# Moving output-block matmuls ahead of two f tiles, and one accumulating DMA over all tap pairs

## The chip, the core and the metric

The kernel runs on one core of a Trainium2 chip. The metric is the device time of one execution in microseconds (us); it is shown as the median of several runs. The core's engines are named as in the profile: PE (TensorE matmuls), PEld (its weight loads), DVE (VectorE), ACT (ScalarE), POOL (GpSimd) and SP (SyncE, which here only issues DMAs). POOL also issues DMAs.

## What is computed

The reference has two stages. Shapes: x is 8 x 4096 x 192, weight_gen is 8 x 4096 x 8 heads x 7 taps, w_in is 192 x 2048, w_out is 2048 x 192, all float32.

```python
w = softmax(weight_gen, axis=taps)                      # 7 taps
out[b, s, h, g] = sum_k w[b, s, h, k] * x_pad[b, s + k, h, g]   # causal, 6 zero rows ahead
h = out.reshape(32768, 192) @ w_in
g = h - np.tanh(h)
result = g @ w_out
```

## The kernel before

The 32,768 tokens are cut into 32 tiles (n = 0 to 31) of 1,024 tokens. A tile passes through these steps, several tiles being in flight at once.

1. **Weights.** SP loads weight_gen (L98) and x with its halo rows (L112). ACT takes the exponential (L145), DVE sums, inverts and scales (L159, L168, L174, L198). The scaling uses a PSUM bank as scratch space.
2. **Products.** `products(n)` (L204) multiplies x with each of the seven taps on POOL (L223). Taps 0, 2, 4 go to the three planes of `even`, taps 1, 3, 5 to the three planes of `odd`, tap 6 to `last`, all bf16. After the planes are written, POOL issues a DMA (L240) that adds `odd` onto `even` in SBUF (`accum_op=add`), so that the next step has fewer groups to add. From which tile on, and how much of the planes, is set by `PLAIN`, `PART` and `ACC` (L46 to L48): tiles 0 and 1 have no DMA; tiles 2 to 5 (`PART`) send it after tap 3 and over two pairs of planes, so that five groups remain (tap 4, two summed pairs, tap 5, tap 6); tiles 6 to 31 send it after tap 5 and over `ACC` = 4,096 of the 4,608 elements of a partition, so that four groups remain and, for the third 64-column chunk of the 192 columns, a fifth: the part of tap 5 that the DMA left out.
3. **Convolution sums.** `conv_sums(n)` (L259) adds the groups on PE by matmuls with an identity (L276), which also transpose, into PSUM: one buffer `pc` for chunks 0 and 1, a second for chunk 2. ACT (L302) and DVE (L300) copy them to SBUF as `convT`, bf16.
4. **First matmul.** `gemm1(n, f)` (L314) makes one of 16 f tiles (128 columns of w_in by 1,024 tokens) by six matmuls (L319) into a PSUM buffer `ph` of two banks. ACT takes the tanh from it into `th` (L330); DVE subtracts (L331) into `gt`, which frees `ph`.
5. **Second matmul.** `gemm2(i, f0, f1)` (L340) makes an output block of 128 tokens as a sum over the f tiles f0 to f1. Its 128-row contraction is split into two row tiles of 64 that run side by side: the first half of block i goes to one of two PSUM banks, `obank0` or `obank1`, and at the same time the second half of block i-1 to the other. So each f tile is two matmuls (L353), and 16 f tiles are 32. When block i-1 is complete, ACT copies it out (L372); the next block that begins in that bank waits for that copy.

In PSUM two banks are the obanks, and three buffers of two banks each form one pool (`psum_h`, bufs=3, L60), which `ph` and `pc` take in turn. A new `ph` or `pc` therefore waits for the buffer that was taken three allocations before it.

The order on each engine is the order in which the code is written (`tc.manual_schedule()`). The main loop (L509 to L573) goes over n from 1. For p = 0 to 7 it writes gemm1 of f tiles 2p and 2p+1 of tile n, then `out_block(n, p)`, which is gemm2 of block p of tile n-1. At p = 6 the convolution sums of tile n+1 are interleaved with the output block. Between p = 6 and p = 7 stand the sums of chunk 2, and then the first two f tiles of output block 7 (`out_block(n, 7, 0, 2)`, L562), f tiles 14 and 15 of gemm1, and the rest of block 7 (L569). At p = 0 `products(n + 2)` is written too; its first product waits for the subtraction of f tile 1 (`behind=last_sub[0]`, "pace").

At i = 1 (the second output block) a manual dependency (L363) makes the first matmul of the second row tile wait for the ACT instruction kept in `g1_act` (L328): the tanh of f tile 2. At the last block there is one like it.

Of the kernel before, what the change touches and what calls it, by code (L numbers as in the profile page):

```python
# [8 lines left out]
FP32 = mybir.dt.float32  # L9
BF16 = mybir.dt.bfloat16  # L10

ACT = mybir.ActivationFunctionType
# [4 lines left out]
def kernel(  # L17
# [8 lines left out]
    nc = tc.nc  # L26

    B, S, D = x.shape
# [3 lines left out]
    P = nc.NUM_PARTITIONS  # L32
    R = P // 2
    HALO = K - 1

    J = 8
# [6 lines left out]
    NC = D // R  # L43
    GC = G // NC
    NPAIR = K // 2
    ACC = NPAIR * J * D - J * R  # L46
    PLAIN = (0, 1)
    PART = (2, 3, 4, 5)  # L48
    assert S % TOK == 0 and D % R == 0 and H * GC == R and F % P == 0
    assert NFT == 2 * J, "one token block of the second matmul per pair of f tiles"  # L50

# [14 lines left out]
    obank = [psum_o.tile([P, 512], FP32, name=f"obank{i}", tag=f"obank{i}") for i in range(2)]  # L66
    zero = const.tile([1, D], FP32, name="zero")
    nc.vector.memzero(zero[:])

    x_of = {}  # L70
    wg_of = {}
# [4 lines left out]
    prods_of = {}  # L76
    conv_of = {}
    g_of = {}
    last_act = {}
    g1_act = {}  # L80
    last_sub = {}
    last_exp = {}
    last_conv = {}
# [2 lines left out]
    def order(inst, other, reason):  # L86
        tc.add_manual_dep(
            inst.ins,
            other.ins.name,
            mybir.DependencyInfo(mybir.DependencyClass.Sync, mybir.DependencyReason.DATA),  # L90
            reason=reason,
        )
# [111 lines left out]
    def products(n, taps=None, sums=None, hooks={}, behind=None):  # L204

        x_t = x_of.pop(n)
        wsm, wsm_v, e_t, zr = wsm_of.pop(n)
        if e_t is not None:
            scale(nc.gpsimd, wsm[:], e_t, zr[:])

        even = ppool.tile([P, NPAIR, NC, J, H, GC], BF16, name="even")
        odd = ppool.tile([P, NPAIR, NC, J, H, GC], BF16, name="odd")
        last = ppool.tile([P, NC, J, H, GC], BF16, name="last")
        dst = {}
        for i in range(NPAIR):
            dst[2 * i] = even[:, i]
            dst[2 * i + 1] = odd[:, i]
        dst[K - 1] = last[:]
        if -1 in hooks:
            hooks[-1]()  # L220
        for eng, k, j0, j1 in taps or [(nc.gpsimd, k, 0, J) for k in range(K)]:
            w = wsm_v if eng is nc.vector else wsm[:]
            mul = eng.tensor_mul(  # L223
                dst[k][:, :, j0:j1].rearrange("p c j h g -> p j h c g"),
                x_t[:, k + j0 : k + j1, :].rearrange("p j (h c g) -> p j h c g", h=H, c=NC),
                w[:, j0:j1, :, k : k + 1]
                .rearrange("p j h (k o) -> p j h k o", o=1)
                .to_broadcast([P, j1 - j0, H, NC, GC]),
            )
            if k == 0 and behind is not None:  # L230


                order(mul, behind, "pace")
            if j1 == 1:
                first_halo[0] = mul
            if (k, n in PART) in ((3, True), (K - 2, False)) and n not in PLAIN:


                acc = 2 * J * D if n in PART else ACC
                nc.gpsimd.dma_start(  # L240
                    out=even[:].rearrange("p i c j h g -> p (i c j h g)")[:, 0:acc],
                    in_=odd[:].rearrange("p i c j h g -> p (i c j h g)")[:, 0:acc],
                    accum_op=mybir.AluOpType.add,
                    max_dma_last_dim=4096,
                )
            if k in hooks:
                hooks[k]()

        if n in PLAIN:
            prods_of[n] = [[dst[k] for k in (sums or range(K))]] * NC  # L250
        elif n in PART:
            prods_of[n] = [[dst[4], even[:, 0], even[:, 1], dst[5], last[:]]] * NC
        else:
            groups = [last[:]] + [even[:, i] for i in range(NPAIR)]
            prods_of[n] = [
                groups + ([odd[:, NPAIR - 1]] if c == NC - 1 else []) for c in range(NC)
            ]

    def conv_sums(n, parts, pcs, home=None):  # L259

# [53 lines left out]
    def gemm1(n, f):  # L314
        convT = conv_of[n]
        ph = psum_h.tile([P, 2, HT], FP32, name="ph", tag="ph")
        for c in range(NC):
            for r in range(2):
                nc.tensor.matmul(  # L319
                    ph[:, r, :],  # L320
                    lhsT=w_in[r * R : (r + 1) * R, c, f * P : (f + 1) * P],
                    rhs=convT[r * R : (r + 1) * R, c, :],
                    start=(c == 0),
                    stop=(c == NC - 1),
                )
        th = tpool.tile([P, TOK], FP32, name="th")
        ph_f = ph[:].rearrange("p r t -> p (r t)")
        g1_act[0] = last_act.get(0)  # L328
        gt = gpool.tile([P, TOK], BF16, name=f"gt{f}", tag=f"gt{f}")
        last_act[0] = nc.scalar.activation(out=th[:], in_=ph_f, func=ACT.Tanh)  # L330
        last_sub[0] = nc.vector.tensor_sub(gt[:], ph_f, th[:])  # L331
        g_of.setdefault(n, []).append(gt)

    LAST = (NTOT - 1) * J
    LEAD = 5
    LATE = (1, 2, 3, 4, 5, 6)
    half = {}
    out_of = {}

    def gemm2(i, f0=0, f1=NFT, between=lambda f: None):  # L340

        ops = []
        for r, blk in ((0, i), (1, i - 1)):
            if not 0 <= blk < LAST:
                continue
            n, j = divmod(blk, J)
            if r == 0 and f0 == 0:
                half[blk] = obank[blk % 2]
            ops.append((r, n, j, half[blk]))
        for f in range(f0, f1):  # L350
            for r, n, j, po in ops:
                col = (j % 2) * HT + (j // 2) * P
                mm = nc.tensor.matmul(  # L353
                    po[:, 0:D],
                    lhsT=g_of[n][f][r * R : (r + 1) * R, col : col + P],
                    rhs=w_out[r * R : (r + 1) * R, f, :],
                    start=(r == 0 and f == 0),
                    stop=(r == 1 and f == NFT - 1),
                )
                if r == 1 and f == 0 and i in (1, LAST):  # L360


                    order(mm, g1_act[0] if i == 1 else last_act[0], "row tiles in one bank")  # L363
            between(f)
        if i > 0 and f1 == NFT:
            blk = i - 1
            n, j = divmod(blk, J)
            po = half.pop(blk)
            if j == 0:
                out_of[n] = opool.tile([P, J, D], FP32, name="out_sb")  # L370
            out_sb = out_of[n]
            last_act[0] = nc.scalar.activation(out=out_sb[:, j, :], in_=po[:, 0:D], func=ACT.Copy)  # L372
            if j == J - 1:
                out_of.pop(n)
                g_of.pop(n)
                nc.sync.dma_start(
                    out=out[n * TOK : (n + 1) * TOK, :].rearrange("(p j) e -> p j e", p=P),
                    in_=out_sb[:],
                )
# [126 lines left out]
    def out_block(n, p, f0=0, f1=NFT, between=lambda f: None):  # L506
        gemm2((n - 1) * J + p, f0, f1, between)

    for n in range(1, NTOT):  # L509
        for p in range(J):  # L510
            more = n < NTOT - 1
            if more and p == 6:
                break
            gemm1(n, 2 * p)
            gemm1(n, 2 * p + 1)
            if n == 1:

                if p == 0:
                    load_wg(5)
                if p <= 1:  # L520
                    softmax_sum(3, p * JH, (p + 1) * JH)
                elif p <= 3:
                    softmax_recip(3, (p - 2) * JH, (p - 1) * JH)
                else:
                    softmax_sum(4, (p - 4) * JH, (p - 3) * JH)
                if p == 2:
                    softmax_exp(4)
                if p == 3:
                    wsm_of[3] = (softmax_tile(), None, e_of[3], zr_of[3])
                    products(3)  # L530
            elif n + 3 < NTOT:
                if p == 0:
                    softmax_exp(n + 3)
                if p == 0 and n + 4 < NTOT:
                    load_wg(n + 4)
                if 1 <= p <= 2:
                    softmax_sum(n + 3, (p - 1) * JH, p * JH)
                if 3 <= p <= 4:
                    softmax_recip(n + 3, (p - 3) * JH, (p - 2) * JH)
            out_block(n, p)  # L540
            if p == 0 and 1 < n < NTOT - 2:
                products(n + 2, behind=last_sub[0])
            if p == 0 and n + 3 < NTOT and n not in LATE:
                load_x(n + 3)
# [14 lines left out]
        some(conv_sums(n + 1, ((2,),), pcs), K * 4 * JH)  # L559


        out_block(n, 7, 0, 2)  # L562
        conv_out(n + 1, ((2,),), pcs, nc.vector)
        if n + 3 < NTOT:

            softmax_norm(n + 3, pcs[0][:, 0])
        gemm1(n, 14)
        gemm1(n, 15)
        out_block(n, 7, 2)  # L569
        if n in LATE:  # L570


# [37 lines left out]
```

## Time and profile before

| what | value |
|---|---|
| median of 7 runs | 756.95 us (756.25 to 758.35) |
| the profiled execution: its own time | 756.88 us |
| its span, first to last instruction | 755.1 us |
| granted TensorE clock | 1.000 |
| busy: PE / DVE / POOL / ACT | 97% / 92% / 89% / 83% of the span |
| idle time of PE in the span | 20.8 us, of which the startup up to 40 us holds nearly all |
| matmuls | 14,784: 7,936 of gemm2 (L353), 3,072 of gemm1 (L319), 3,520 of the sums (L276), 256 of the last tile's own output (L390) |
| DMAs `even<-odd` | 26 of 1,024 KB and 4 of 768 KB |

The span is what lies between the first and the last instruction; the execution's own time is 1.8 us longer. A busy PE is not a PE at its peak: a matmul's busy time includes its passage through the pipeline, so short waits of PE do not show as idle time. They show as a longer distance between the starts of two matmuls.

### The profile page before, as it was taken

The numbers are of one execution on the slowest core, as the hardware profiler recorded it, in microseconds if no ns is written. First come the engines' busy times: TensorE is split into PE (matmuls) and PEld (weight loads), VectorE is DVE, ScalarE is ACT, GpSimd is POOL, SyncE is SP. The second block draws the span as 40 slices with busy tenths as digits, with TensorE's granted clock in tenths as the row PEclk, the third lists the DMA queues.
The fourth block names the chain that finished last, engine by engine and source line by source line (L and its number), as shares of the span: only waits on it lengthen the run. The fifth ranks groups of instructions, "written<-read, shape, count | busy, mean of one in ns | idle before, by whom it ended". The sixth has DMA issues, their size and how long they took to land.

```text
span 755.1 us, 32326 instructions
## 1 busy us (share of the span) xinstructions
PE 734.3 (97%) x14784; PEld 579.0 (77%) x14784; DVE 695.5 (92%) x740; ACT 625.1 (83%) x839; POOL 670.7 (89%) x264
## 2 busy tenths in 40 slices
PE   3899999999999999999999999999999999999997
PEld 2487878877777877787878777777777777777777
DVE  7989999999999999999999999999999999998893
ACT  4888888888888888888888888888888888888883
POOL 8999999999999999999999999999999999999000
PEclk9999999999999999999999999999999999999999
DMA  8935444466546665554666544666544666542312
GB/s 229 221 67 172 154 146 107 124 185 179 159 136 170 185 184 143 138 137 148 179 185 172 117 133 149 172 185 184 113 130 149 169 185 173 123 111 63 79 45 86
DMA packets 25943, 111.08 MB, mean 147 GB/s; under 512 B 4703, under 2 KB 9551, under 8 KB 21838
## 3 DMA queue, kind: packets, MB, share of 16 engines
q1 hardware_dynamic: 14718, 77.03, 28.3%
q0 software_dynamic: 11088, 31.99, 24.8%
q8 instruction: 115, 1.88, 1.0%
q14 instruction: 22, 0.18, 0.1%
HBM read 54.52 MB, written 25.17 MB: 106 GB/s over the span
## 4 chain that ended last, share of the span: by engine, by line
PE 80%; POOL 17%; DMA 2%; issue 1%; ACT 0%; DVE 0%; POOLq 0%
PE obank L353 37%; PE ph L319 36%; POOL even L223 7%; POOL odd L223 6%; PE pc L276 5%; POOL last L223 2%; PE po L390 1%; DMA even<-odd 1%; POOL wsm L198 0%; POOL w_in L432 0%; DMA wg_t<-in_weight_gen_dram 0%; POOL even L240 0%; POOL w_out L419 0%; ACT e_t L145 0%; DVE out_sb L404 0%
## 5 line engine op out<-in xcount | busy, mean ns | idle before, releaser
L331 DVE TENSOR_TENSOR gt<-ph,th 128x1024 bf16<-128x1024 f32 x512 | 602.4, 1219 | 35.4 <-ACT th L330 32.5
L330 ACT ACTIVATE th<-ph 128x1024 f32<-128x1024 f32 x512 | 497.3, 1022 | 71.8 <-PE ph L319 69.0
L353 PE MATMUL obank<-w_out,gt 64*128 64x192 bf16 x7936 | 407.9, 243 | 0.6 <-ACT th L330 0.4
L353 PEld LDWEIGHTS <-gt 64*128 64x128 bf16 x7936 | 356.4, 94 | 49.7 <-ACT th L330 0.8
L319 PE MATMUL ph<-convT,w_in 64*128 64x512 bf16 x3072 | 385.1, 378 | 4.6 <-DVE gt L331 2.5
L223 POOL TENSOR_TENSOR even<-x_t,wsm 128x1536 bf16<-128x1536 f32 x93 | 285.1, 3065 | 15.2 <-DVE gt L331 15.0
L223 POOL TENSOR_TENSOR odd<-x_t,wsm 128x1536 bf16<-128x1536 f32 x93 | 284.8, 3062 | 0.0
L319 PEld LDWEIGHTS <-w_in 64*128 64x128 bf16 x3072 | 177.5, 94 | 108.3 <-issue 19.5
L372 ACT ACTIVATE out_sb<-obank 128x192 f32<-128x192 f32 x248 | 82.0, 331 | 36.8 <-PE obank L353 30.0
L223 POOL TENSOR_TENSOR last<-x_t,wsm 128x1536 bf16<-128x1536 f32 x32 | 106.7, 3334 | 0.0
L276 PE MATMUL pc<-ident,even 64*128 64x64 bf16 x2256 | 63.0, 192 | 1.2 <-DMA even<-odd 0.9
L276 PEld LDWEIGHTS <-even 64*128 64x128 bf16 x2304 | 60.0, 96 | 2.3 <-DMA even<-odd 1.0
L240 POOL DMA_DIRECT2D even<-odd x30 | 36.1, 1205 | 9.3 <-POOL odd L223 9.3
L276 PE MATMUL pc<-ident,last 64*128 64x64 bf16 x752 | 27.4, 191 | 9.2 <-POOL last L223 9.2
L302 ACT ACTIVATE convT<-pc 128x1024 bf16<-128x1024 f32 (+1 forms) x33 | 32.7, 993 | 2.8 <-PE pc L276 2.8
L276 PEld LDWEIGHTS <-last 64*128 64x128 bf16 x768 | 23.5, 96 | 9.4 <-POOL last L223 9.2
L159 DVE TENSOR_REDUCE zsum<-e_t 128x32 f32<-128x224 f32 (+1 forms) x61 | 23.7, 388 | 2.9 <-ACT e_t L145 2.9
L300 DVE CAST convT<-pc 128x512 bf16<-128x512 f32 x30 | 20.7, 690 | 4.5 <-PE pc L276 2.8
L145 ACT ACTIVATE e_t<-wg_t 128x448 f32<-128x448 f32 x32 | 18.5, 577 | 6.7 <-DMA wg_t<-in_weight_gen_dram 6.7
L168 DVE RECIPROCAL zr<-zsum 128x32 f32<-128x32 f32 (+1 forms) x58 | 20.3, 350 | 0.0
L198 DVE TENSOR_TENSOR wsm<-e_t,pc 128x448 f32<-128x448 f32 x28 | 17.4, 622 | 2.9
L276 PE MATMUL pc<-ident,odd 64*128 64x64 bf16 x400 | 14.5, 199 | 1.1 <-POOL odd L223 0.7
(28 smaller groups left out, 77.1 us busy)
## 6 DMA issues: line engine op xcount, KB each, us to landing
x_t<-in_x_dram SPq DMA_DIRECT2D x31, 1344.0 KB, 9.5
even<-odd POOLq DMA_DIRECT2D x26, 1024.0 KB, 8.9
out_dram<-out_sb SPq DMA_DIRECT2D x31, 768.0 KB, 7.3
wg_t<-in_weight_gen_dram SPq DMA_DIRECT2D x32, 224.0 KB, 9.9
even<-odd POOLq DMA_DIRECT2D x4, 768.0 KB, 7.4
x_t<-in_x_dram SPq DMA_DIRECT2D x1, 768.0 KB
w_out<-in_moe_w_out_dram POOLq DMA_DIRECT2D x1, 768.0 KB, 8.8
out_dram<-out_sb SPq DMA_DIRECT2D x4, 192.0 KB, 2.6
```

The costliest lines, as they stand in the source:

```text
L159: nc.vector.reduce_sum(out=zsum_of[n][:, j0 * H : j1 * H], in_=e_of[n][:, j0:j1].rearrange("p j h k -> p (j h) k"), axis=AX.X,)
L168: nc.vector.reciprocal(zr_of[n][:, j0 * H : j1 * H], zsum_of[n][:, j0 * H : j1 * H])
L223: mul = eng.tensor_mul(dst[k][:, :, j0:j1].rearrange("p c j h g -> p j h c g"), x_t[:, k + j0 : k + j1, :].rearrange("p j (h c g) -> p j h ...
L240: nc.gpsimd.dma_start(out=even[:].rearrange("p i c j h g -> p (i c j h g)")[:, 0:acc], in_=odd[:].rearrange("p i c j h g -> p (i c j h g)" ...
L276: nc.tensor.matmul(pc[r][:, col : col + R] if home else pc[:, r, col : col + R], lhsT=prods[c][gi][r * R : (r + 1) * R, c, 2 * j : 2 * j + ...
L300: eng.tensor_copy(out, pc[:, :, 0:cols].rearrange("p r (cj t) -> p r cj t", t=R))
L302: last_conv[0] = nc.scalar.activation(out=out, in_=pc[:, :, 0:cols].rearrange("p r (cj t) -> p r cj t", t=R), func=ACT.Copy,)
L319: nc.tensor.matmul(ph[:, r, :], lhsT=w_in[r * R : (r + 1) * R, c, f * P : (f + 1) * P], rhs=convT[r * R : (r + 1) * R, c, :], start=(c == ...
L330: last_act[0] = nc.scalar.activation(out=th[:], in_=ph_f, func=ACT.Tanh)
L331: last_sub[0] = nc.vector.tensor_sub(gt[:], ph_f, th[:])
L353: mm = nc.tensor.matmul(po[:, 0:D], lhsT=g_of[n][f][r * R : (r + 1) * R, col : col + P], rhs=w_out[r * R : (r + 1) * R, f, :], start=(r == ...
L372: last_act[0] = nc.scalar.activation(out=out_sb[:, j, :], in_=po[:, 0:D], func=ACT.Copy)
```

## The change

Four things change.

- `FILL`: ahead of f tile 14, four f tiles (eight matmuls) of output block 7 instead of two.
- `AHEAD`: from n = 2 on, three f tiles (six matmuls) of output block 0 stand between f tiles 0 and 1 of gemm1; the other 13 follow f tile 1.
- The accumulating DMA covers all three pairs of planes in tiles 7 to 31, as three pieces of 1,536 elements per partition where there were two of 2,048; the fifth group of chunk 2 goes. Tile 6 moves from this kind to `PART`.
- The manual dependency at i = 1 waits for a new ACT instruction (`probe`), which copies one column of the `ph` of f tile 2 and stands ahead of that tile's tanh.

```diff
-    ACC = NPAIR * J * D - J * R
     PLAIN = (0, 1)
-    PART = (2, 3, 4, 5)
+    PART = (2, 3, 4, 5, 6)
...
-                acc = 2 * J * D if n in PART else ACC
+                pairs = 2 if n in PART else NPAIR
                 nc.gpsimd.dma_start(
-                    out=even[:].rearrange("p i c j h g -> p (i c j h g)")[:, 0:acc],
-                    in_=odd[:].rearrange("p i c j h g -> p (i c j h g)")[:, 0:acc],
+                    out=even[:, 0:pairs].rearrange("p i c j h g -> p i (c j h g)"),
+                    in_=odd[:, 0:pairs].rearrange("p i c j h g -> p i (c j h g)"),
...
-            groups = [last[:]] + [even[:, i] for i in range(NPAIR)]
-            prods_of[n] = [
-                groups + ([odd[:, NPAIR - 1]] if c == NC - 1 else []) for c in range(NC)
-            ]
+            prods_of[n] = [[last[:]] + [even[:, i] for i in range(NPAIR)]] * NC
...
-        g1_act[0] = last_act.get(0)
         gt = gpool.tile([P, TOK], BF16, name=f"gt{f}", tag=f"gt{f}")
+        if n == 1 and f == 2:
+
+            probe[0] = nc.scalar.activation(out=once[:], in_=ph_f[:, 0:1], func=ACT.Copy)
...
+    FILL, AHEAD = 4, 3
...
-                    order(mm, g1_act[0] if i == 1 else last_act[0], "row tiles in one bank")
+                    order(mm, probe[0] if i == 1 else last_act[0], "row tiles in one bank")
...
             gemm1(n, 2 * p)
+            ahead = AHEAD if p == 0 and n > 1 else 0
+            if ahead:
+                out_block(n, p, 0, ahead)
             gemm1(n, 2 * p + 1)
...
-            out_block(n, p)
+            out_block(n, p, ahead)
...
-        out_block(n, 7, 0, 2)
+        out_block(n, 7, 0, FILL)
         conv_out(n + 1, ((2,),), pcs, nc.vector)
...
         gemm1(n, 14)
         gemm1(n, 15)
-        out_block(n, 7, 2)
+        out_block(n, 7, FILL)
```

More of the change, by code (lines that the diff above doesn't have):

```diff
@@ L68 @@
     nc.vector.memzero(zero[:])
+    once = const.tile([P, 1], FP32, name="once")
     x_of = {}
@@ L79 @@
     last_act = {}
-    g1_act = {}
+    probe = {}
     last_sub = {}
```

## The prediction

> **What bounds the kernel now.** I read the page's busy table first (PE 97%, DVE 92%, POOL 89%), then the waits, then the timeline of one period of the main loop, because PE's waits of under 0.1 us are too short for the waits view. By the chain of waits (PE 80%, POOL 17%) the end is set by PE. One pass of the main loop takes 22.56 us: f tile 14 starts at 489.83 in the timeline below and at 512.39 one pass later. In the waits two lines matter, a small one for PE and a large one for POOL, which is early every pass and waits for the "pace" dependency:
>
> ```profile
> PE ph L319 <- DVE gt L331: 2.5, 7, 0.6
> POOL even L223 <- DVE gt L331: 15.0, 17, 0.9
> ```
>
> The timeline around the boundary of tiles n=20 and 21 (start, length, engine, line, tiles, count) shows every step that the change touches:
>
> ```profile
> 488.56 1.22 DVE L331 TENSOR_TENSOR gt<-ph,th 128x1024 bf16<-128x1024 f32 x1
> ...
> 489.05 0.30 PE L276 MATMUL pc<-ident,last 64*128 64x64 bf16 x8
> ...
> 489.17 0.53 PE L276 MATMUL pc<-ident,even 64*128 64x64 bf16 x24
> 489.21 0.33 ACT L372 ACTIVATE out_sb<-obank 128x192 f32<-128x192 f32 x1 [0.90 <-PE obank L353]
> 489.44 1.02 ACT L302 ACTIVATE convT<-pc 128x1024 bf16<-128x1024 f32 x1
> ...
> 489.52 0.30 PE L276 MATMUL pc<-ident,odd 64*128 64x64 bf16 x8
> ...
> 489.63 0.34 PE L353 MATMUL obank<-w_out,gt 64*128 64x192 bf16 x4
> ...
> 489.83 1.50 PE L319 MATMUL ph<-convT,w_in 64*128 64x512 bf16 x12
> ...
> 490.69 1.94 ACT L330 ACTIVATE th<-ph 128x1024 f32<-128x1024 f32 x2 [0.24 <-PE ph L319]
> ...
> 491.15 1.33 PE L353 MATMUL obank<-w_out,gt 64*128 64x192 bf16 x28
> ...
> 491.75 3.70 DVE L331 TENSOR_TENSOR gt<-ph,th 128x1024 bf16<-128x1024 f32 x3 [0.22 <-ACT th L330]
> ...
> 492.31 1.55 PE L319 MATMUL ph<-convT,w_in 64*128 64x512 bf16 x12
> ...
> 492.52 0.33 ACT L372 ACTIVATE out_sb<-obank 128x192 f32<-128x192 f32 x1
> ...
> 493.03 0.33 PEld L319 LDWEIGHTS <-w_in 64*128 64x128 bf16 x5 [0.20 <-issue]
> ...
> 493.67 1.50 PE L353 MATMUL obank<-w_out,gt 64*128 64x192 bf16 x32
> ...
> 494.99 0.40 PE L319 MATMUL ph<-convT,w_in 64*128 64x512 bf16 x2
> ```
>
> To be seen: distances between starts give PE's true price. 28 gemm2 matmuls take 492.31 - 491.15 = 1.16, so 0.0412 each; an f tile of six takes 0.645 (493.67 - 493.03); 40 matmuls of the sums take 489.63 - 489.05 = 0.58, 0.0145 each. What exceeds this is waiting. F tile 14 starts 0.05 after the subtraction that ends at 488.56 + 1.22 = 489.78; the four fill matmuls would let it start at 489.80, so it waits 0.03. F tile 15 starts at 490.51, 0.05 after L302's copy ends (490.46): 0.03. F tile 1 starts at 493.03, where 492.31 + 0.645 = 492.955 was possible: 0.07, 0.05 after the subtraction of f tile 14 ends (491.75 + 1.22 = 492.97). In all 0.13 per pass.
>
> **Removed matmuls and the two fills, per pass.** From tile 7 on, chunk 2 loses 8 of 40 matmuls, 8 x 0.0145 = 0.12. With the 0.13 of waits 0.24 would be on offer. I follow PE through the new order.
> - The sums end at 489.51. The fill starts in the bank that ACT's L372 reads until 489.54; 0.05 later, 489.59. That read was just covered before; now 0.08 of the 0.12 goes into waiting for it.
> - Eight fill matmuls, 0.33: f tile 14 at 489.92, 0.09 later than now. Its buffer is free (489.83). F tile 15 at 490.565 (free at 490.51). 24 matmuls from 491.21: f tile 0 at 492.20, 0.11 earlier than now.
> - The new fill could start at 492.845. But it begins output block 0 in the bank of block 6 of the tile before, which L372 reads. On ACT that copy is queued behind the two tanh of f tiles 14 and 15: now the first tanh starts 0.86 after f tile 14, L372 1.83 after the tanh, and L372 lasts 0.33. With f tile 14 at 489.92: tanh 490.78, L372 492.61 to 492.94, PE 492.99. A new wait of 0.145, where the old one was 0.07.
> - Six matmuls, 0.25: f tile 1 at 493.24 (its buffer is free at 493.11). 26 matmuls from 493.885: the next pair of f tiles at 494.96 instead of 494.99.
>
> So a pass gains **0.03**: the fills cover the waits for DVE, and two waits for ACT's copies take their place. Behind the new wait on PE stand f tile 1 and the rest of block 0; they are not late, since six matmuls are done. DVE is not late either: its subtraction of f tile 0 is freed about 0.1 earlier. The 25 boundaries of n=6 to 30 give 25 x 0.03 = 0.8. Those of n=2 to 5 have 40 matmuls in chunk 2 before and after; the same walk leaves nothing.
>
> **POOL and the DMA.** The larger DMA has three pieces per partition instead of two. The issue costs POOL 1.20 us (L240, mean 1,205 ns) with two pieces in both sizes, and 1,231 ns with sixteen (w_out, L419). So a third costs nothing, at most in proportion 0.60; it can't gain. The pace wait of 0.93 covers either. Landing has two rows:
>
> ```profile
> even<-odd POOLq DMA_DIRECT2D x26, 1024.0 KB, 8.9
> even<-odd POOLq DMA_DIRECT2D x4, 768.0 KB, 7.4
> ```
>
> 1.5 us for 256 KB; the added 128 KB cost 0.75 (between 0 and, if each piece counted, half of 8.9, 4.5). In late passes the DMA is issued 18.7 before PE needs it: nothing. It counts on tile 7. The Trainium skill, "DMA: Bandwidth & Descriptors", section "Anatomy of one DMA — SWDGE (gpsimd) path", prices such a DMA at 2.0 us plus bytes over 436,000 per us: an estimate of 0.3 for 128 KB, and 4.4 in all for 1,024 KB, where this trace shows 8.9, so I don't use it; by it the total below would be 2.2 instead of 1.7.
>
> **The ramp.** PE on tiles 6 and 7, POOL, and the second output block:
>
> ```profile
> 147.51 0.28 PE L276 MATMUL pc<-ident,last 64*128 64x64 bf16 x3
> 148.71 0.20 PE L276 MATMUL pc<-ident,even 64*128 64x64 bf16 x2 [0.93 <-DMA even<-odd]
> ```
> ```profile
> 160.54 1.20 POOL L240 DMA_DIRECT2D even<-odd  x1 [0.30 <-POOL odd L223]
> ```
> ```profile
> 171.24 0.21 PE L276 MATMUL pc<-ident,even 64*128 64x64 bf16 x2
> ```
> ```profile
> 41.72 0.24 PE L353 MATMUL obank<-w_out,gt 64*128 64x192 bf16 x1
> ...
> 42.36 1.49 PE L353 MATMUL obank<-w_out,gt 64*128 64x192 bf16 x31 [0.39 <-ACT th L330]
> ```
>
> - The first sums of `even` of tile 6 come 1.2 late (148.71; on tile 7 they come 0.40 after the first of `last`, which on tile 6 would be 147.54). With `PART` the DMA is issued two products earlier and the last product ends at 143.1: the wait of 1.17 goes, and 16 more matmuls come (80 instead of 64 for chunks 0 and 1), 0.23.
> - The manual wait at 41.74 lasts 0.61. The probe, one column, takes by the slope of ACT's rows (192 columns 0.33, 1,024 columns 1.02) 0.17, at most 0.33, and ends before 41.70: 0.6 gained, less at most 0.1 for a later tanh.
> - PE would then reach tile 7's `even` at 171.24 - 1.17 + 0.23 - 0.6 - 0.1 (small gains at n=1 to 5) = 169.6. What is late next is tile 7's own DMA: POOL issues it at 160.54 as before (POOL is there at its own pace, 21.56 per tile, and `PART` has the same products and one DMA), now for 1,152 KB: this one landed after 9.0, so 9.75 now, 170.29, and PE goes on at 170.34. PE loses 0.7 of its lead: **0.9** remains. If the size cost nothing, 1.6 would remain; with 10.4, 0.25.
>
> **Sum.** 0.9 + 0.8 = 1.7: span 753.4, the profiled execution 756.88 - 1.7 = 755.2. It stands at the median (756.95), so the time is **755.2**.
>
> **Rivals.**
> 1. *The fills cover everything.* If ACT's copies don't bind, f tile 14 starts at 489.85 and the pass gains 0.235: 25 x 0.235 + 0.9 = 6.8, 750.1. For: every DVE wait does go. Against: the order on ACT and the bank; it needs the copy of block 6 to end by 492.79, and it ends at 492.85 already now. 0.08.
> 2. *The boundary gives 0.06 to 0.1* (my walk's error being as large as the 0.07 that PE waits today): 752.8 to 754.2. 0.13.
> 3. *Nothing to measure.* A boundary gives 0 or loses 0.02, and tile 7's DMA takes most of the ramp: 0.25 - 0.5 at the worst, 755.6 to 757.2. 0.26.
> 4. *Slower: tile 7 waits long for the DMA.* The slowest landing in this trace is 12.9 (issued at 246.75). With the 0.75, on tile 7, it lands at 174.2: 3.0 later than PE came before, less 0.8: 759.1. Slower by over 0.2% from a landing of 13 us on. For: the wait at tile 6 shows that this place has no slack; PE now comes 9.1 after the issue. Against: tiles 6 to 9 landed in 8.7 to 9.7. 0.05.
>
> **The numbers.** 0.2% (1.5 us) is about what a measurement of this kernel can tell from no change; faster means under 755.4, slower over 758.5. My forecast (754.3 to 755.9) has 0.48: 0.32 of it faster, 0.16 the same. Faster: 0.32 + 0.08 + 0.13 = 0.53; same: 0.16 + 0.26 = 0.42; slower 0.05. The range takes in the forecast and rivals 2 and 3, 752.8 to 757.2, and leaves out 0.13.
>
> **What would show it.** A pass of 22.53 in the timeline; six matmuls of block 0 that start 0.05 after L372 ends, 0.79 after f tile 0; f tile 14 with no wait; no wait of PE for the DMA at tile 6, one of about 0.7 near 170; L240's successor at 1.2 us; 14,600 matmuls (200 less, 16 more); POOL still waiting about 0.9 for its pace. I am wrong if the fill of block 0 starts without a wait (rival 1), or if POOL's wait is gone.

## The result: slower by 0.28%, and the profile after

| what | before | after |
|---|---|---|
| median of the runs shown | 757.34 us (756.25 to 759.66, 62 runs) | 759.57 us (758.01 to 762.00, 26 runs) |
| ratio, 95% interval | | 1.0028 [1.0023, 1.0034] |
| profiled execution: own time / span | 756.88 / 755.1 us | 759.83 / 758.1 us |
| granted TensorE clock in it | 1.000 | 0.997 |
| matmuls | 14,784 | 14,600 |

The forecast was 755.2 and its range ended at 757.2; the time is 2.4 us outside. The profiled executions differ by 3.0 us. To see where, take the same event of each tile in the PE timeline of both kernels: the first sum of an `even` plane that the DMA has added to (L276 before, L272 after), called the sum of the tile below.

| sum of tile | 6 | 7 | 8 | 9 | 10 | 31 |
|---|---|---|---|---|---|---|
| before, us | 148.71 | 171.24 | 193.97 | 216.89 | 239.45 | 713.31 |
| after, us | 147.60 | 170.42 | 196.30 | 220.35 | 243.19 | 716.32 |
| after - before | -1.11 | **-0.82** | +2.33 | +3.46 | **+3.74** | **+3.01** |

Read it in three parts. Up to tile 7 the change has gained 0.82. From tile 10 to 31 it gains 0.73 in 21 passes, 0.035 each. Between tiles 7 and 10 it loses 4.56, and that is the result.

**The steady passes.** Timeline of the changed kernel at the boundary of tiles 20 and 21 (start, length, engine, line, tiles, count), the counterpart of the stretch shown before:

```profile
492.50 0.53 PE L272 MATMUL pc<-ident,even 64*128 64x64 bf16 x24
492.54 0.33 ACT L372 ACTIVATE out_sb<-obank 128x192 f32<-128x192 f32 x1 [0.90 <-PE obank L353]
...
492.92 0.51 PE L353 MATMUL obank<-w_out,gt 64*128 64x192 bf16 x8
...
493.25 1.47 PE L315 MATMUL ph<-convT,w_in 64*128 64x512 bf16 x12
...
494.55 1.17 PE L353 MATMUL obank<-w_out,gt 64*128 64x192 bf16 x24
...
495.54 0.83 PE L315 MATMUL ph<-convT,w_in 64*128 64x512 bf16 x6
...
495.94 0.34 ACT L372 ACTIVATE out_sb<-obank 128x192 f32<-128x192 f32 x1
...
496.32 0.42 PE L353 MATMUL obank<-w_out,gt 64*128 64x192 bf16 x6
...
496.57 0.83 PE L315 MATMUL ph<-convT,w_in 64*128 64x512 bf16 x6
```

The sums would let the fill of f tile 14 start at 492.85; it starts at 492.92, 0.05 after L372's copy ends (492.54 + 0.33). F tile 0 lasts 0.645, so the fill of block 0 could start at 496.18; it starts at 496.32, 0.05 after the second copy ends (495.94 + 0.34). Both fills wait for ACT, as the prediction walked it.

**Tiles 7 to 10.** The waits of the changed kernel (who waited for whom: sum, times, longest):

```profile
POOL even L223 <- DVE gt L329: 13.3, 17, 0.8
...
PE pc L272 <- DMA even<-odd: 3.2, 1, 3.2
...
POOL odd L223 <- DMA even<-odd: 2.6, 1, 2.6
```

The last two are single events, and the last has no counterpart before: a *product* on POOL waits for an accumulating DMA. POOL's timeline of the changed kernel shows where:

```profile
160.47 1.28 POOL L239 DMA_DIRECT2D even<-odd  x1 [0.30 <-POOL odd L223]
161.29 3.40 POOL L223 TENSOR_TENSOR last<-x_t,wsm 128x1536 bf16<-128x1536 f32 x1
164.16 3.38 POOL L223 TENSOR_TENSOR even<-x_t,wsm 128x1536 bf16<-128x1536 f32 x1
170.19 2.90 POOL L223 TENSOR_TENSOR odd<-x_t,wsm 128x1536 bf16<-128x1536 f32 x1 [2.64 <-DMA even<-odd]
...
184.83 1.29 POOL L239 DMA_DIRECT2D even<-odd  x1 [0.30 <-POOL odd L223]
```

Before, the same stretch has no stop, and the DMA of tile 8 goes out 2.74 earlier:

```profile
164.18 3.35 POOL L223 TENSOR_TENSOR even<-x_t,wsm 128x1536 bf16<-128x1536 f32 x1
167.04 3.34 POOL L223 TENSOR_TENSOR odd<-x_t,wsm 128x1536 bf16<-128x1536 f32 x1
...
182.09 1.20 POOL L240 DMA_DIRECT2D even<-odd  x1 [0.30 <-POOL odd L223]
```

Tile 7's DMA (issued 160.47) lands 9.64 later, at 170.11, and only then does POOL write the first `odd` product of tile 8. Tile 8's own DMA, issued 2.74 late at 184.83, takes 11.43 (8.67 before), and PE stands still for it. PE's timeline of the changed kernel, then the windows view of the three stretches (window, length, busy us and counts of PE, PEld, DVE, ACT, POOL; then the granted clock, DMA share and GB/s):

```profile
192.90 0.24 PE L272 MATMUL pc<-ident,last 64*128 64x64 bf16 x4
196.30 0.20 PE L272 MATMUL pc<-ident,even 64*128 64x64 bf16 x2 [3.17 <-DMA even<-odd]
196.34 0.30 PE L353 MATMUL obank<-w_out,gt 64*128 64x192 bf16 x2
196.43 0.37 PE L272 MATMUL pc<-ident,even 64*128 64x64 bf16 x6
196.61 0.35 PE L353 MATMUL obank<-w_out,gt 64*128 64x192 bf16 x2
196.75 0.37 PE L272 MATMUL pc<-ident,even 64*128 64x64 bf16 x6
```
```profile
192.90:196.30 3.40, 0.24 (x13) 0.11 (x6) 2.15 (x2) 0.67 (x1) 3.40 (x2) 1.00 0.99 330
196.40:199.80 3.40, 3.40 (x100) 3.32 (x100) 0.00 (x0) 0.88 (x2) 3.40 (x2) 0.50 0.37 148
199.80:203.20 3.40, 3.40 (x54) 2.20 (x50) 2.77 (x5) 2.53 (x5) 3.40 (x3) 1.00 0.02 5
```

PE stands still for 3.36 from the last matmul of `last` to the first of `even`. (Waits of PE are given like this, from start to start; the profile's idle time in brackets leaves out the length of the matmul before, about 0.2.) Then the granted clock is 0.50 for 3.4 us: the interleaved groups come every 0.32 (196.43 to 196.75) where they come every 0.17 at full clock. From tile 8 to 9 this makes 24.05 in place of 22.53, another 1.5. With a stop of 0.4 in tile 9's pass (22.84 in place of 22.53) the three passes hold 5.2 us too much; before they held 0.5 too much (22.73, 22.92 and 22.56, against 22.56), and three times 0.03 is gained. That leaves the 4.56.

**Why POOL waits there.** `odd` has two buffers. The placement in the built programs, A and B for the two addresses (a profile holds no addresses; what the traces show is that of the tiles from 2 to 31 only tile 8's first `odd` product waits for the DMA of the tile before, in the changed kernel, and none before):

```
tile        4  5  6  7  8  9 10
before      A  B  A  B  A  B  A
after       A  B  A  B  B  A  B
```

The changed kernel gives tile 8 the buffer that tile 7 has just used. Read against the code, the reason is who reads `odd` last. Before, from tile 6 on, the fifth group of chunk 2 reads the `odd` plane of tap 5 on PE, and tiles 2 to 5 (`PART`) read tap 5 on PE as well: always PE, always in tile order. In the changed kernel tile 6 is still read last by PE in its sums, but tile 7, the first with the DMA over all pairs, is read last by its DMA, which the code writes before the sums of tile 6. So tile 7's buffer is free first in program order, and the next request gets it. In time it is the buffer that is free last. After this one exchange the order alternates again. This rule is read from the code, but three runs below fit it: with the larger DMA from tile 6 on (dma_only) the stop moves to tile 7, as was expected of it beforehand, and where PE still reads tap 5 (part6_only, small_fill3) there is none.

**POOL and DMA rows of the page after**:

```profile
L239 POOL DMA_DIRECT2D even<-odd x30 | 38.2, 1275 | 9.2 <-POOL odd L223 9.2
```
```profile
even<-odd POOLq DMA_DIRECT2D x25, 1152.0 KB, 9.4
...
even<-odd POOLq DMA_DIRECT2D x5, 768.0 KB, 7.6
```

The third piece costs POOL 0.08 per tile (1.28 against 1.20; the pitch of the DMA issues goes from 21.55 to 21.63), and the landing grows by 0.5 in the median (8.9 to 9.4). At tiles 8 to 12 it is 11 to 15 (8.7 to 12.9 before).

### The profile page after: what moved, and what is told of

It reads as the page before. It is cut to its first block, busy times and chain, and to the rows that moved or that the text cites. A ratio compares the mean times of both kernels' runs of the same rounds, so it can differ in the third digit from the quotient of the medians.

```text
span 758.1 us, 31929 instructions
## 1 busy us (share of the span) xinstructions
PE 735.2 (97%) x14600; PEld 575.3 (76%) x14600; DVE 692.4 (91%) x740; ACT 628.0 (83%) x840; POOL 672.9 (89%) x264
## 4 chain that ended last, share of the span: by engine, by line
PE 74%; POOL 22%; DMA 2%; issue 2%; ACT 0%; DVE 0%; POOLq 0%
PE obank L353 35%; PE ph L315 33%; POOL even L223 9%; POOL odd L223 9%; PE pc L272 5%; POOL last L223 3%; DMA even<-odd 2%; PE po L390 1%; POOL w_in L432 0%; POOL wsm L198 0%; POOL even L239 0%; DMA wg_t<-in_weight_gen_dram 0%; POOL w_out L419 0%; ACT e_t L145 0%; DVE out_sb L404 0%
## 5 line engine op out<-in xcount | busy, mean ns | idle before, releaser
L353 PE MATMUL obank<-w_out,gt 64*128 64x192 bf16 x7936 | 413.0, 243 | 0.0
L315 PEld LDWEIGHTS <-w_in 64*128 64x128 bf16 x3072 | 174.1, 94 | 100.5 <-issue 10.4
L372 ACT ACTIVATE out_sb<-obank 128x192 f32<-128x192 f32 x248 | 81.9, 330 | 38.9 <-PE obank L353 34.6
L272 PE MATMUL pc<-ident,even 64*128 64x64 bf16 x2256 | 64.2, 193 | 3.7 <-DMA even<-odd 3.2
L272 PEld LDWEIGHTS <-even 64*128 64x128 bf16 x2304 | 61.0, 97 | 4.6 <-DMA even<-odd 3.3
L239 POOL DMA_DIRECT2D even<-odd x30 | 38.2, 1275 | 9.2 <-POOL odd L223 9.2
L272 PE MATMUL pc<-ident,last 64*128 64x64 bf16 x752 | 27.0, 192 | 9.1 <-POOL last L223 9.1
L272 PEld LDWEIGHTS <-last 64*128 64x128 bf16 x768 | 23.1, 96 | 9.3 <-POOL last L223 9.1
L390 PE MATMUL po<-w_out,gt 64*128 64x192 bf16 x256 | 11.2, 243 | 0.0
```

The lines of the kernel that those rows point to most:

```text
L239: nc.gpsimd.dma_start(out=even[:, 0:pairs].rearrange("p i c j h g -> p i (c j h g)"), in_=odd[:, 0:pairs].rearrange("p i c j h g -> p i (c ...
L272: nc.tensor.matmul(pc[r][:, col : col + R] if home else pc[:, r, col : col + R], lhsT=prods[c][gi][r * R : (r + 1) * R, c, 2 * j : 2 * j + ...
L315: nc.tensor.matmul(ph[:, r, :], lhsT=w_in[r * R : (r + 1) * R, c, f * P : (f + 1) * P], rhs=convT[r * R : (r + 1) * R, c, :], start=(c == ...
L353: mm = nc.tensor.matmul(po[:, 0:D], lhsT=g_of[n][f][r * R : (r + 1) * R, col : col + P], rhs=w_out[r * R : (r + 1) * R, f, :], start=(r == ...
```

## Experiments

Theory: the exchange of `odd` buffers at tile 8 is the loss; the rest of the change gains what was forecast. Rivals: the larger DMA itself (its landing and its third piece) is the loss, or the fills are. Ratios are against before, with 95% intervals, five rounds each; "sum of tile n" is as above.

**1. `odd` by parity (parity).** The changed kernel with two named buffers for `odd`.

```diff
+    oddpool = ctx.enter_context(tc.tile_pool(name="oddpool", bufs=1))
...
-        odd = ppool.tile([P, NPAIR, NC, J, H, GC], BF16, name="odd")
+        slot = n % 2
+        odd = oddpool.tile([P, NPAIR, NC, J, H, GC], BF16, name=f"odd{slot}", tag=f"odd{slot}")
```

> The changed kernel with one edit: the buffer of odd is taken by the tile's parity, as it was before the change, so that tile 8 no longer takes the buffer of tile 7. Slot theory (tile 8's first odd product waits for the landing of tile 7's DMA, POOL loses 2.6 us, tile 8's DMA is issued late, PE waits 3.4 us and its clock halves for 3.4 us): POOL's wait near 167 us goes, tile 8's DMA is issued at about 182.1 instead of 184.8, PE's wait at tile 8 falls under 0.6 us, no clock drop, and the time is that of the recorded forecast, 1.2 to 2.0 us under the kernel before (ratio 0.9974 to 0.9984). Size theory (the three-piece DMA lands late by itself, 11.4 us at tile 8 where 8.7 was): PE still waits 0.6 us or more there, and if the landing grows as it did, the time stays within 0.5 us of the kernel before. Fill theory (the moved matmuls cost): the time stays where the changed kernel is, 2 us over the kernel before.

Measured: 756.59, ratio **0.9989** [0.9980, 0.9998], 2.9 us under the changed kernel. POOL's stop is gone and tile 8's DMA goes out at 182.19:

```profile
167.10 3.38 POOL L225 TENSOR_TENSOR odd<-x_t,wsm 128x1536 bf16<-128x1536 f32 x1
...
182.19 1.29 POOL L241 DMA_DIRECT2D even<-odd  x1 [0.30 <-POOL odd L225]
```

PE still waits 1.1 at tile 8, because this DMA lands after 11.26, and the clock stays at 1.00 behind this shorter wait:

```profile
192.34 0.24 PE L274 MATMUL pc<-ident,last 64*128 64x64 bf16 x4
193.49 0.20 PE L274 MATMUL pc<-ident,even 64*128 64x64 bf16 x2 [0.91 <-DMA even<-odd]
```

So without the exchange the change is faster than before, by 0.8 us of the 1.7 that were forecast. The expectation had under 0.6 for this wait and a ratio of 0.9974 to 0.9984 if the exchange were all: both missed, because the later landing at tile 8 remains.

**2. The exchange put back (swap_at8, swap_at10, swap_late).** The own pool also moves buffers to other places in SBUF. These three keep it and turn the parity round from one tile on:

```diff
-        slot = n % 2
+        slot = n % 2 if n < 8 else (n + 1) % 2     # swap_at8; 10 and 20 in the others
```

> The kernel with `odd` in its own two buffers by parity, and the exchange put back by hand at tile 8: from there on the parity is turned round, so that tile 8 takes tile 7's buffer, as the pool gave it in the changed kernel. Everything else, the places of the buffers too, is as in the parity run. Theory (the exchange at this tile is the loss): GpSimd stops for 2.6 us ahead of tile 8's first odd product, the DMA of tile 8 goes out near 184.8 in place of 182.2, TensorE waits 3 to 3.7 us there in place of 1.1, and the time is again that of the changed kernel, ratio 1.002 to 1.004 against 0.999 with parity. Rival (the places of the buffers, or something else that the own pool changed, made the gain): no change from the parity run, 0.998 to 1.000.

> The same with the exchange at tile 10. Theory: what it costs is worked out from the parity run's rows: tile 10's first odd product is due at 210.4, tile 9's DMA lands at 203.84 + 11.69 = 215.5, so GpSimd stops for 5.1 us; tile 10's DMA goes out at 230.6 in place of 225.5 and lands 12.2 later at 242.8; TensorE came there at 239.2, so it waits 3.6 us (with landings between 9 and 14 us: 0.4 to 5.4). Ratio near 0.999 + 0.005 = 1.004, and up to 1.006 if the granted clock falls after the wait as it did in the changed kernel. Rival: since the exchange at tile 20 (a stop and a landing of 11.5 us) cost nothing, one at tile 10, where TensorE uses the sums 13.7 us after the issue in place of 9.3 to 11.3, costs under 1 us: ratio 0.999 to 1.000.

> As parity, but the exchange of the two odd buffers that the changed kernel makes at tile 8 is put at tile 20: tile 20 takes the buffer of tile 19. Slot theory, with its place: POOL waits about 2.6 us again at tile 20's first odd product, but PE needs the summed planes there some 18 us after the issue, twice the landing, and POOL makes the loss good from its pace wait of 0.9 us a tile: the time equals that of parity within 0.4 us. Rival (a stop of POOL costs its length wherever it falls): 2.6 us more than parity.

| exchange at tile | POOL's stop | DMA of that tile goes out / lands after | sum comes after the issue | PE waits | ratio |
|---|---|---|---|---|---|
| none (parity; tile 8) | 0 | 182.19 / 11.26 | 11.31 | 1.10 | 0.9989 [0.9980, 0.9998] |
| 8 | 2.09 | 184.30 / 11.19 | 11.23 | 2.77 | **1.0042** [1.0028, 1.0055] |
| 10 | 3.66 | 229.47 / 10.94 | 10.98 | 0.31 | 1.0023 [1.0014, 1.0033] |
| 20 | 0.88 | 447.96 / 11.54 | 17.51 | 0 | 0.9996 [0.9987, 1.0005] |

At tile 8 the loss is back, as large as in the changed kernel or larger, with the buffers in the places of the parity run: the exchange is the cause, not the places. The stop and the late issue, in the trace of swap_at8:

```profile
169.66 2.90 POOL L225 TENSOR_TENSOR odd<-x_t,wsm 128x1536 bf16<-128x1536 f32 x1 [2.09 <-DMA even<-odd]
...
184.30 1.29 POOL L241 DMA_DIRECT2D even<-odd  x1 [0.30 <-POOL odd L225]
```

This profiled execution, the fastest of five (758.43), has no stretch of half clock after the 2.77 wait. It is 1.5 over parity's (756.91), about what the longer wait adds (2.77 - 1.10 = 1.67), so this much of the loss needs no clock; what the other four (758.93 to 761.34) lose beyond it is open. At tile 20 the exchange costs nothing that shows: PE comes 17.5 after the issue even so, and its sums of tiles 19 and 20 are both 0.06 behind parity's. POOL's stop there is only 0.88, though, where 2.6 was expected. At tile 10 it costs too, 0.0034 above parity (2.6 us), against the rival's "under 1 us"; but the theory's sum of 3.6 of waiting is not confirmed. In the profiled execution POOL stops for 3.66 and not 5.1 (tile 9's DMA landed after 10.66), tile 10's DMA has landed at 240.41 and not 242.8, and PE comes 0.9 later than in parity, because of a stop of 1.50 at 217.8 that no semaphore ends; so 0.31 of waiting is left. A second such stop, 1.66 at 264.6, which parity doesn't have, makes up most of the rest. That the exchange brings these stops about is not shown: parity_fill3, without any exchange, has one of 1.50 too. What they are is in the last section.

**3. The DMA alone (dma_only, dma_only_parity).** Before, with the DMA over all pairs and without the fifth group (the two hunks of the diff on `ACC`, `pairs` and `groups`); `PART` stays 2 to 5, no fills, no probe. The second adds `odd` by parity as in experiment 1.

> The kernel before with the accumulating DMA over all pairs alone; tiles 2 to 5 keep the partial kind. Slot theory: the exchange of the odd buffers moves to tile 7, which takes the buffer of tile 6; its first odd product is due at 145.5 and tile 6's DMA lands at about 149.2, so POOL loses about 3.7 us, tile 7's DMA is issued near 164.2 and lands near 173.8, and PE, due at 171.7, waits about 2 us; with 0.5 us for the later landing of tile 6's DMA and nothing saved in a pass (f tile 14 is held by the subtraction of f tile 13 in any case) the time is 2 to 3.5 us over the kernel before, more if the clock drops. Size theory: 0.5 us over the kernel before.

> The larger accumulating DMA alone (PART 2 to 5, no fills, no probe), as in the run with that part alone, but `odd` takes its buffer by the parity of the tile. If the exchange of `odd` buffers makes the loss of that run (its ratio was 1.0035, 3 us), the stop of GpSimd for the DMA of the tile before goes (3.1 us on the first odd product of tile 7), TensorE's waits for DMA at tiles 6 to 8 (1.9, 1.0 and 1.3 us) fall to about 1.7 at tile 6 (the 1.17 of before and half a microsecond for the larger transfer) and under 1.1 at tiles 7 and 8, and the time lies within 0.8 us of before (ratio 0.999 to 1.001). The rival, that the larger transfer itself makes it (longer landings, the third piece's 0.08 us per tile on GpSimd), expects the ratio to stay at 1.003.

Measured: 760.41, ratio **1.0035** [1.0022, 1.0049], and 757.59, ratio **1.0005** [0.9997, 1.0014]. Here tile 6 is the first with all pairs and tile 7 takes its buffer. Waits of dma_only:

```profile
PE pc L272 <- DMA even<-odd: 3.7, 3, 1.7
...
POOL odd L222 <- DMA even<-odd: 3.1, 1, 3.1
```

and of dma_only_parity, where one wait is left, at tile 6 (1.67 from start to start, about the 1.17 of before and the half microsecond of the larger transfer):

```profile
PE pc L274 <- DMA even<-odd: 1.5, 1, 1.5
```

The exchange moves with the first such tile, and 2.3 us go when it is taken away (by the ratios; 2.8 by the medians). The larger DMA by itself makes no measurable difference. It gains nothing in the steady passes: one is 22.565, as before (22.56), although four column groups of two matmuls, 0.12, are gone. The sums end at 490.54 there (tile 20), the fill starts at 490.62, 0.05 after L372's copy: 0.08 of waiting; and f tile 14 waits 0.045 longer than before for its subtraction. That is the 0.12.

**4. The fills alone (fills_only).** Before, with `FILL, AHEAD = 4, 3` and its two places in the loop.

> The kernel before with the two fills alone (four and three f tiles). My walk (waits for ACT's copies of the output banks take the place of the waits for DVE): f tile 14 starts about 0.13 us later in a pass, f tile 1 waits behind the copy of block 6, and a pass is 22.55 instead of 22.56: 0 to 0.3 us gained, no measurable change. Rival (the fills cover all slot waits): 0.13 us a pass, 3 to 4 us gained. Fill theory (they cost): slower by 1 us or more.

Measured: 758.4, ratio 1.0011 [1.0002, 1.0020]; a pass is 22.58, where 22.55 was expected. The fills take the DVE waits away and get ACT's copies in their place, and without the removed group there is nothing left over: the prediction's first rival (0.235 per pass) is refuted. The 0.02 per pass makes 0.5 us; the rest of the 0.8 is inside the interval.

**5. The ramp's two parts (part6_only, probe_only).**

```diff
-    PART = (2, 3, 4, 5)
+    PART = (2, 3, 4, 5, 6)
```

> Before, with tile 6 as the fifth of the tiles whose DMA takes two pairs; nothing else. It goes by the step of the prediction for the ramp: the wait of 1.17 us for tile 6's DMA goes, 16 more matmuls cost 0.23, and tile 7's DMA (8.9 us landing in before) must not be late instead. Expected 0.9 us less than before, ratio 0.9988, tile 7's first even product summed near 170.3. The rival, that a transfer limits each of the tiles 7 to 9 anyway, expects a wait at tile 7 or 8 that gives the 0.9 back: ratio 1.000. The `odd` buffers: tile 7 is again the first of the larger transfers, so an exchange as in the changed kernel is possible here too, and would show as a stop of GpSimd of 2 to 3 us at tile 8 and a ratio over 1.002; it is not expected where the last pair's odd product is still read by TensorE, as in before.

> Before, with the one-column ScalarE copy as the order point of the first output block; nothing else. The stall of 0.64 us near 41.7 us goes, tiles 2 to 5 run 0.6 us earlier, and the wait for tile 6's DMA near 148.7 grows from 1.2 to 1.8 us, since that DMA hangs on GpSimd and not on TensorE: no change, ratio 1.000 within 0.0005. The rival, that GpSimd's start of each tile is paced by the same TensorE chain (by the subtraction that it waits for), has the DMA earlier by 0.6 as well and the ratio at 0.9992.

Measured: part6_only 756.4, ratio **0.9991** [0.9983, 1.0000]: the wait at tile 6 is gone, and tile 7's sum is at 170.66 (170.3 was expected) with its DMA landed at 169.57, so no other wait took its place; at tile 31 its profiled execution is 0.37 ahead (712.94), the medians 1.0. No exchange of buffers there, since PE still reads tap 5. probe_only (only the probe's hunks): 757.36, ratio **1.0000** [0.9991, 1.0009]; PE stood still 1.43 for tile 6's DMA where it was 1.12, and tile 6's sum came at 148.59 against 148.71: the wait swallowed the gain. So the probe is worth something only with tile 6 in `PART`; the move of tile 6 gains without the probe.

**6. Three and three (parity_fill3, small_fill3, late_fill3).** By the rows at the boundary, the fourth f tile of `FILL` delays f tile 14 and with it the copy that the fill of block 0 waits for. The first is the parity run with

```diff
-    FILL, AHEAD = 4, 3
+    FILL, AHEAD = 3, 3
```

> The changed kernel with `odd` by the tile's parity, and three f tiles ahead of f tile 14 in place of four. By the rows of the changed kernel: the fill of f tile 14 ends its wait for the bank copy with two matmuls less behind it, and the fill ahead of f tile 1 then waits 0.04 for its bank copy in place of 0.145, so a pass takes 22.44 us in place of 22.53. That makes 25 x 0.09 = 2.3 us less than the parity run (ratio 0.9989): 754.4 us, ratio 0.996. The rival, that the waits for the banks move and do not go (as the two fills did: 22.53 against 22.56), expects 22.5 to 22.56 and a ratio of 0.998 to 0.999.

Measured: 754.91, ratio **0.9967** [0.9956, 0.9979]; a pass is 22.45. Timeline of its boundary of tiles 20 and 21:

```profile
488.49 0.53 PE L274 MATMUL pc<-ident,even 64*128 64x64 bf16 x24
488.92 0.42 PE L355 MATMUL obank<-w_out,gt 64*128 64x192 bf16 x6
489.16 1.49 PE L317 MATMUL ph<-convT,w_in 64*128 64x512 bf16 x12
490.47 1.25 PE L355 MATMUL obank<-w_out,gt 64*128 64x192 bf16 x26
491.55 0.83 PE L317 MATMUL ph<-convT,w_in 64*128 64x512 bf16 x6
492.24 0.42 PE L355 MATMUL obank<-w_out,gt 64*128 64x192 bf16 x6
492.48 0.83 PE L317 MATMUL ph<-convT,w_in 64*128 64x512 bf16 x6
```

F tile 14 starts 0.24 after its fill (0.33 in the changed kernel), and the fill of block 0 starts 0.69 after f tile 0, where 0.645 was possible (0.79 in the changed kernel). The other two ask what of the larger DMA is worth having. small_fill3 is before with `PART` to 6, the probe and fills of three and three, and the old DMA. late_fill3 is parity_fill3 with the old DMA and group up to tile 14, and all pairs only from tile 15 on (`FULL = 15`).

> All of the change except the larger DMA: before's DMA and sums, tile 6 as the fifth of the two-pair tiles, the probe, and fills of three and three f tiles. The ramp gets 0.9 (tile 6 alone gave 0.9) and the probe's 0.6 on top, as no DMA wait swallows it any more; a pass takes 22.58 (fills of four and three alone) less 0.08 (what three and three gave with the larger DMA) = 22.50, against 22.56: 25 x 0.06 = 1.5. Together 3.0 us less than before, ratio 0.996. Theory: the larger DMA is the part that costs (waits of 0.3 and 1.0 us at tiles 7 and 8 and a gap of 1.5 at tile 9 with it), so this kernel has none of these three, and its tile 10 starts near 237.5 us against 239.7 in the kernel with both. Rival: the gaps at tiles 9 and 10 come with any DMA there, and the ratio is 0.997 to 0.998.

> The changed kernel with `odd` by parity, fills of three and three, and the larger DMA only from tile 15 on; tiles 7 to 14 keep before's DMA and sums. Theory: the larger DMA costs at tiles 7 to 10 alone, where its landing is not covered (9 to 11 us between issue and use; from tile 15 on there are 18), and saves its four matmuls a pass where it is covered: waits of 0.3 and 1.0 and the 1.5 gap of the kernel with the larger DMA everywhere go (2 us, since the gaps partly remain in before too), 7 passes cost 0.05 more: 753 us, ratio 0.9945. Rival: the four matmuls' 0.12 a pass go into the waits for the banks also late, and the time equals that of the kernel with the small DMA everywhere.

| run | sum of tile 7 / 8 / 10 | PE waits for DMA at 7 and 8 | pass, tiles 20 to 21 | median | ratio |
|---|---|---|---|---|---|
| parity_fill3 | 169.90 / 193.37 / 239.67 | 0.34, 0.99 | 22.45 | 754.91 | 0.9967 [0.9956, 0.9979] |
| small_fill3 | 170.05 / 192.97 / 238.51 | 0, 0.43 | 22.50 | 754.67 | 0.9963 [0.9952, 0.9975] |
| late_fill3 | 169.66 / 192.16 / 238.76 | 0, 0 | 22.45 | 753.85 | 0.9960 [0.9946, 0.9973] |

All three are faster than before by 0.33 to 0.40%, and faster than the changed kernel. late_fill3 has the waits of none and the pass of the better, and by the median it is the fastest, but the three intervals overlap, so the order among them is open. Its expectation of 753 missed by the stop of PE at tile 9, which was 1.24 here with the small DMA (0.45 in small_fill3): that stop does not need the larger DMA, as the expectation had it (it is one of those in the last section).

## Why the prediction was wrong

- **The pass: right.** 22.53 forecast, 22.53 measured, by the two waits for ACT's copies that were named (0.05 behind L372, 0.79 behind f tile 0); 0.035 per pass from tile 10 on against 0.03. That is 0.7 of 0.8.
- **Tile 6 and the probe: right; tile 7: right in the number, by luck.** The DMA wait at tile 6 and the 0.64 stop at 41.72 are gone. Tile 7's sum comes at 170.42 where 170.34 was forecast, and 0.82 of the forecast 0.9 was in hand at this point. But the forecast wait of 0.7 is not there: the DMA landed at 170.11 (after 9.64; 9.75 was forecast), ahead of PE. PE, forecast for 169.6, came 0.8 later by itself: the startup of this execution is 0.3 longer, and the pass from tile 5 to the first sum of tile 6 takes 23.15 where part6_only, without fills, takes 22.78. The 0.1 of small gains at n=1 to 5 didn't come either (tile 2 to tile 5: 68.45, before 68.41).
- **POOL's third piece: mis-sized, without effect.** "So a third costs nothing": it costs 0.08 per tile, inside the bound, and POOL's pace wait (0.8, before 0.9) covers it.
- **The step that failed** is the one on POOL: "POOL is there at its own pace, 21.56 per tile, and `PART` has the same products and one DMA". It counts POOL's instructions and not what they wait for. It holds at tile 7 (issue at 160.47) and fails at tile 8, where POOL's `odd` product waits 2.64 for the DMA of tile 7. The diff takes away PE's read of `odd` from tile 7 on; that read was priced as eight matmuls of 0.0145 to be saved, and it was also what kept the two buffers in turn. The prediction asked for the price of each operation and never for who reads each buffer last. Neither of its two signs of being wrong came (the fill of block 0 did wait, and POOL still waits 0.8 for its pace): both watch the steady pass, and the loss is in the ramp.
- **A second term, the landing at tile 8.** "Landing" was taken at tile 7 and carried no further. At tile 8 the larger transfer took 11.4, and 9.6 to 11.4 in all kernels that have it there (8.7 to 10.1 for the smaller one). Even without the exchange this leaves a wait of 1.1 in parity, 0.99 in parity_fill3, none in dma_only_parity. In parity's profiled execution this wait and two stops of PE at tiles 9 and 10 (0.74 and 0.90, below) take back all that was gained (756.91 against 756.88); by the medians 0.8 of the forecast 1.7 is left.
- **Rival 4** had the right sign, place (a tile of the ramp waits long for its DMA) and size (759.1), for another reason: it needed a landing of 13 us, and got a DMA that went out 2.7 late and landed after 11.4. With only a slow landing to trigger it, 0.05 was its chance; the buffer was the mechanism that the list lacked. (Rival 2's upper end is 0.3 too low: 25 x 0.06 + 0.9 = 2.4 gives 754.5 and not 754.2; nothing hangs on it.)

## What to carry to other kernels

When a change removes or moves the last reader of a buffer that rotates, work out again which buffer the next tile gets: by the placements here the pool chooses by the order of the program, and what is free first in the program may be free last in time. Name the slots by parity where the rotation matters. And follow a gain in the ramp past the first tile: a wait that is gone at tile 6 says nothing of tile 8, where the next transfer has its own landing and its own lead.

## What the runs showed of the hardware that was not expected

- **The granted clock falls behind a wait of PE.** After 3.36 us of standing still it was 0.50 for 3.41 us (1.5 us lost); after waits of 1.1 (parity), 1.9 (dma_only) and 2.77 (swap_at8) it stayed at 1.00. The Trainium skill, "TensorE: Matmul & The Clock Gate", "What's actually happening", has the clock at half after at least one idle window of about 3.4 us; these four rows agree. The startup has rows that no single long stop explains: in five profiled executions (parity, parity_fill3, dma_only, swap_at8, swap_at10) the clock is 0.50 for 3.41 us from 16.0 to 16.7 on. In parity, in the 3.41 us before that, PE was busy for 1.33, and its longest stop near there is 1.08. Such a stretch takes 0.0023 off a run's mean clock (3.41 x 0.5 / 758), so ten runs of the changed kernel, with means of 0.999 and 1.000, had none; their median is 758.87, 1.5 over before. So about 1.5 of the 2.2 us of the medians come without a stretch of half clock; what it adds in the other runs is open.
- **An accumulating DMA of one size lands after 8.7 to 15.2 us.** In steady passes of parity_fill3 1,152 KB takes 8.7 to 11.2; at tiles 10 to 12 of parity 12.0 to 15.2.
- **PE stops without a releaser, always at the same place of an instruction block.** 13 of the 14 profiled executions have one to three stops of PE of 0.4 to 1.7 us that end with no semaphore (20 in all, counted from 60 us on): 18 between 192 and 267 us, two in probe_only at 332 and 536. The line after one, in late_fill3:

```profile
217.67 0.24 PE L284 MATMUL pc<-ident,last 64*128 64x64 bf16 x5 [1.05 <-issue]
```

They come with the larger DMA (parity 0.74 and 0.90, swap_at10 1.50 and 1.66) and with the smaller one (late_fill3 1.24, small_fill3 0.45, before 0.41). What PE waited for can be counted in the traces. The DMA queue named "instruction" (q8) moves packets of 16,384 bytes, 115 of them before, for PE's 29,568 matmuls and weight loads, and 114 in the changed kernel, for 29,200: one for 256 instructions. At each of the 20 stops the number of PE's recorded instructions so far leaves the same rest when divided by 256, 193 (192 in one): 7,105 in before, 8,129 in late_fill3 and parity, 9,921 in swap_at10. And each ends 1.2 to 1.6 us after such a packet is through; in late_fill3 it starts at 215.30 and takes 0.94, and PE goes on at 217.67. So PE stands there for its next block of instructions. This is read from counts and times; no run here moves these loads, and why some come late is not shown.
